# A decode block's down projection in row form over four column groups, with its residual kept as four rows

## The chip, the cores and the metric

One core of one Trainium2 chip. The metric is the device time of one execution in microseconds (us), lowest is best. The program is one launch. Inside an execution, the profile gives times from the start of the span. All runs quoted here are in the fast state unless said otherwise; executions of the kernel before lie between 412.1 and 412.9 us, apart from occasional ones at 413.1 to 413.8 us (see the last experiments), so differences of 0.1 to 0.3 us between times say little by themselves.

Some words used below: a *packet* is one record of a DMA engine (for a large load, one partition's row); a load is *usable* at the last increment of its semaphore; *PE* is TensorE, *DVE* VectorE, *ACT* ScalarE, *SPq* the queue of SyncE; the *granted clock* is the share of TensorE's full clock that the profile shows.

## The reference

One token goes through a pre-layernorm attention block with a cached KV of 65,536 positions and then a gated feed-forward block:

```python
h  = x + attention(layernorm(x), k_cache, v_cache, wq, wo)   # 32 query heads, 4 KV heads, Dh = 128
h2 = h + (gelu(layernorm(h) @ w_gate) * (layernorm(h) @ w_up)) @ w_down   # D = 1024, F = 3584
```

Everything is bfloat16 in memory. 173 MB are read once, of which 134 MB are the two caches and 22 MB the three feed-forward matrices. The output is one row of 1024 values.

## The kernel before

All large tensors pass through five rotating load buffers of 32 KB a partition, filled by one queue (SyncE's). The tail of the kernel, which the change rewrites:

```python
def load(src, name):                       # every large load: one DMA into a rotating buffer
    t = chpool.tile([P, CW], BF16, name=name, tag="ch")      # 5 buffers of 32768 bytes a partition
    ...
x_row = const.tile([DC, P], BF16, name="x_row")              # x as 8 rows, transposed to x_cp at the start
...
def pair_mm(bank, stat, w2, c, first, last):                 # two 512-column matmuls of a row block
    for s in range(DS):
        g = 2 * s + c % 2
        nc.tensor.matmul(bank[32 * g:32 * g + 32, :], lhsT=stat, rhs=w2[:, s * 512:(s + 1) * 512],
                         start=first, stop=last, tile_position=(0, 32 * g))
...
h_cp = cp_sum(at_r, x_cp, "h_cp")          # residual in column form: h[j*128+p] in partition p, column j
...
for sz in [14, 7, 4, 2, 1]:                # down weights: 28 row blocks in 5 loads
    wv = load(wd_v[:, c0:c0 + sz, :], "wd_sb")
    for cc in range(sz):
        c = c0 + cc
        if c < 14:
            pair_mm(d_ps, actz[:, c, :], wv[:, cc, :], c, c < 2, c + 2 >= 14)
            continue
        for j in range(8):                 # weights stationary, one column moving
            nc.tensor.matmul(dl_ps[:, j:j + 1], lhsT=wv[:, cc, j * P:(j + 1) * P], rhs=act_bf[:, c:c + 1], ...)
    if c0 == 14:                           # after the first load: rows to columns, plus the residual
        nc.vector.tensor_copy(out=d_r[:], in_=d_ps[:])
        hd_cp = cp_sum(d_r, h_cp, "hd_cp")
h2_cp = dl_ps + hd_cp                      # then transpose to 8 rows, cast, one store of 8 rows
nc.sync.dma_start(out=out[0, 0].rearrange("(c p) -> c p", p=P), in_=o_row[:])
```

Of the kernel before, what the change touches and what calls it, by code (L numbers as in the profile page):

```python
# [9 lines left out]
ALU = mybir.AluOpType  # L10
AX = mybir.AxisListType
BF16 = mybir.dt.bfloat16
F32 = mybir.dt.float32
# [4 lines left out]
def kernel(  # L18
# [13 lines left out]
    nc = tc.nc  # L32
    P = 128
    D = A_x.shape[-1]
# [5 lines left out]
    DC = D // P  # L40
    FC = F // P
# [18 lines left out]
    const = ctx.enter_context(tc.tile_pool(name="const", bufs=1))  # L60
    small = ctx.enter_context(tc.tile_pool(name="small", bufs=2))
    chpool = ctx.enter_context(tc.tile_pool(name="chpool", bufs=NBUF))
    ps_m = ctx.enter_context(tc.tile_pool(name="ps_m", bufs=1, space=PSUM))
# [10 lines left out]
    def load(src, name):  # L74
        t = chpool.tile([P, CW], BF16, name=name, tag="ch")
        n, w = src.shape[1], src.shape[2]
        tv = t[:, 0:n * w].rearrange("p (n w) -> p n w", w=w)
        nc.sync.dma_start(out=tv, in_=src)
        return tv
# [3 lines left out]
    assert HD <= CW and DC % WB == 0  # L83
    x_pc_bf = const.tile([P, DC], BF16, name="x_pc_bf")
    nc.scalar.dma_start(out=x_pc_bf[:], in_=A_x[0, 0].rearrange("(p c) -> p c", c=DC))
    x_row = const.tile([DC, P], BF16, name="x_row")
    nc.scalar.dma_start(out=x_row[:], in_=A_x[0, 0].rearrange("(c p) -> c p", p=P))
    wq_tiles = []
    for c0 in range(0, DC, WB):
        wv = load(wq_v[:, c0:c0 + WB, :], "wq_sb")  # L90
        wq_tiles.extend(wv[:, i, :] for i in range(WB))

    ident_bf = const.tile([P, P], BF16, name="ident_bf")
    make_identity(nc, ident_bf[:])
    ident_f = const.tile([P, P], F32, name="ident_f")
# [3 lines left out]
    hsel = const.tile([P, 2], F32, name="hsel")  # L99
# [43 lines left out]
    nc.vector.tensor_copy(out=x_pc[:], in_=x_pc_bf[:])  # L143
    xn_bf = const.tile([P, DC], BF16, name="xn_bf")
    layernorm_cols(x_pc[:], xn_bf[:], "ln1")
    xT_ps = ps_m.tile([P, DC], BF16, name="xT_ps", tag="misc")
    nc.tensor.transpose(out=xT_ps[:], in_=x_row[:], identity=ident_bf[0:DC, 0:DC])
    x_cp = const.tile([P, DC], F32, name="x_cp")
    nc.vector.tensor_copy(out=x_cp[:], in_=xT_ps[:])

    def padded(pool, vec, ncols, name):
        t = pool.tile([P, ncols, 32], BF16, name=name)
        nc.gpsimd.memset(t[:], 0.0)
        nc.vector.tensor_copy(out=t[:, :, 0], in_=vec)
        return t

    def wide_mm(banks, stat, mov, ns, first, last):
        for s in range(ns):
            g = s % 4
            nc.tensor.matmul(banks[s // 4][32 * g:32 * g + 32, :], lhsT=stat, rhs=mov(s),  # L160
                             start=first, stop=last, tile_position=(0, 32 * g))

    def evac(dst, src, k):
        if k % 2 == 0:
            nc.vector.tensor_copy(out=dst, in_=src)  # L165
        else:
            nc.scalar.copy(out=dst, in_=src)  # L167
# [20 lines left out]
    for hf in range(2):  # L188
        for t in range(2):
            o = W2 * hf + rep * t  # L190
            nc.vector.tensor_copy(out=qsel[64 * t:64 * t + 64, :, :, hf, o:o + rep],
                                  in_=qsel_ps[64 * t:64 * t + 64, :, :].rearrange("p a (g h) -> p g a h", h=rep))
# [149 lines left out]
    for dq in range(OQ):  # L342
        nc.tensor.matmul(o2_ps[:], lhsT=osel[:, dq, :], rhs=o_sb[:, dq * Hq:(dq + 1) * Hq],
                         start=(dq == 0), stop=(dq == OQ - 1))

    actx.close()
    rows = ctx.enter_context(tc.tile_pool(name="rows", bufs=1))
    ps_w = ctx.enter_context(tc.tile_pool(name="ps_w", bufs=4, space=PSUM))
    ps_t = ctx.enter_context(tc.tile_pool(name="ps_t", bufs=3, space=PSUM))
    DS = D // 512  # L350

    def row_bank(name):
        return ps_w.tile([P, 512], F32, name=name, tag="w")

    def pair_mm(bank, stat, w2, c, first, last):
# [4 lines that stand above are left out]
# [6 lines left out]
    for wc in range(Hq // WN):  # L366
        wv = load(wo_v[:, wc * WN:(wc + 1) * WN, :], "wo_sb")
        for cc in range(WN):
            c = wc * WN + cc
            pair_mm(at_ps, o2z[:, c, :], wv[:, cc, :], c, c < 2, c + 2 >= Hq)  # L370
    at_r = rows.tile([P, 512], F32, name="at_r")
    nc.vector.tensor_copy(out=at_r[:], in_=at_ps[:])
    hc_ps = ps_t.tile([P, DC], F32, name="hc_ps", tag="T")
    for s in range(DS):
        for c in range(DC):
            nc.tensor.matmul(hc_ps[64 * s:64 * s + 64, c:c + 1], lhsT=at_r[:, c::DC], rhs=hsel[:, s:s + 1],
                             start=True, stop=True, tile_position=(0, 64 * s))
# [3 lines left out]
    layernorm_cols(h_pc[:], hn_bf[:], "ln2")  # L381
    hnz = padded(rows, hn_bf[:], DC, "hnz")

    def cp_sum(row, add, name):
        ps = ps_t.tile([P, 4, DS], F32, name=name + "_ps", tag="T")
        for b in range(4):
            nc.tensor.matmul(ps[:, b, :], lhsT=row[:, b * P:(b + 1) * P], rhs=hsel[:], start=True, stop=True)
        t = rows.tile([P, DC], F32, name=name)
        nc.vector.tensor_tensor(out=t[:].rearrange("p (s b) -> p b s", b=4), in0=ps[:],
                                in1=add[:].rearrange("p (s b) -> p b s", b=4), op=ALU.add)  # L390
        return t

    h_cp = cp_sum(at_r, x_cp, "h_cp")

    assert F <= CW and FC == 28
    GB = CW // F
    NF = FC // 4

    def up_proj(wmat, name, sizes):
        banks = [row_bank(name + "_ps") for _ in range(2)]  # L400
        wv_all = wmat.rearrange("(p c) n -> p c n", c=DC)
        c0 = 0
        for sz in sizes:
            wv = load(wv_all[:, c0:c0 + sz, :], name + "_sb")
            for cc in range(sz):
                c = c0 + cc
                wide_mm(banks, hnz[:, c, :],
                        lambda s, w=wv[:, cc, :]: w.rearrange("p (m j) -> p m j", j=FC)[:, :, 4 * s:4 * s + 4],
                        NF, c == 0, c == DC - 1)
            c0 += sz  # L410
        assert c0 == DC
        outs = []
        for k in range(2):
            ng = min(4, NF - 4 * k)
            ev = rows.tile([P, 512], F32, name=name + "_ev", tag=f"ev{k}")
            evac(ev[0:32 * ng, :], banks[k][0:32 * ng, :], k)
            t_ps = ps_t.tile([P, 4, P], F32, name=name + "_t", tag="T")
            for b in range(4):
                nc.tensor.transpose(out=t_ps[:, b, 0:32 * ng], in_=ev[0:32 * ng, b::4],
                                    identity=ident_f[0:32 * ng, 0:32 * ng])  # L420
            outs.append((16 * k, 4 * ng, t_ps[:, :, 0:32 * ng:32]))
        return outs

    def by_j(t, j0, nj):
        return t[:, j0:j0 + nj].rearrange("p (g b) -> p b g", b=4)
# [11 lines left out]
    gl = rows.tile([P, FC], F32, name="gl")  # L437
    nc.vector.tensor_tensor(out=gl[:], in0=th[:], in1=g_ap[:], op=ALU.mult)
    act_bf = rows.tile([P, FC], BF16, name="act_bf")
    for j0, nj, src in up_proj(B_w_up, "wu", [GB] * (DC // GB - 1) + [GB - 1, 1]):  # L440
        nc.vector.tensor_tensor(out=by_j(act_bf, j0, nj), in0=src, in1=by_j(gl, j0, nj), op=ALU.mult)

    wd_v = B_w_down.rearrange("(p c) n -> p c n", p=P)
    sizes = [14, 7, 4, 2, 1]
    assert sum(sizes) == FC
    NW = sizes[0]
    actz = padded(rows, act_bf[:, 0:NW], NW, "actz")
    d_ps = row_bank("d_ps")
    dl_ps = ps_w.tile([P, DC], F32, name="dl_ps", tag="w")
    nc.vector.memset(dl_ps[:], 0.0)  # L450
    c0 = 0
    for sz in sizes:
        wv = load(wd_v[:, c0:c0 + sz, :], "wd_sb")
        for cc in range(sz):
            c = c0 + cc
            if c < NW:
                pair_mm(d_ps, actz[:, c, :], wv[:, cc, :], c, c < 2, c + 2 >= NW)
                continue
            for j in range(DC):
                nc.tensor.matmul(dl_ps[:, j:j + 1], lhsT=wv[:, cc, j * P:(j + 1) * P], rhs=act_bf[:, c:c + 1],  # L460
                                 start=False, stop=False, skip_group_check=True)
        c0 += sz
        if c0 == NW:
            d_r = rows.tile([P, 512], F32, name="d_r")
            nc.vector.tensor_copy(out=d_r[:], in_=d_ps[:])
            hd_cp = cp_sum(d_r, h_cp, "hd_cp")
    h2_cp = rows.tile([P, DC], F32, name="h2_cp")
    nc.vector.tensor_tensor(out=h2_cp[:], in0=dl_ps[:], in1=hd_cp[:], op=ALU.add)
    h2T_ps = ps_t.tile([DC, P], F32, name="h2T_ps", tag="T")
    nc.tensor.transpose(out=h2T_ps[:], in_=h2_cp[:], identity=ident_f[:])  # L470
    o_row = rows.tile([DC, P], BF16, name="o_row")
    nc.vector.tensor_copy(out=o_row[:], in_=h2T_ps[:])
    nc.sync.dma_start(out=out[0, 0].rearrange("(c p) -> c p", p=P), in_=o_row[:])


# [28 lines left out]
```

## Time and profile before

412.35 us (three runs, 412.24 to 412.71); the profiled execution took 412.36 us, its span is 410.5 us.

| what | reading | where |
|---|---|---|
| load queue busy | 98.1% of 16 DMA engines' span, 422 GB/s | queue table of the page |
| last down weights usable | 406.89 us | last semaphore increment of that load |
| last down matmul ends | 407.33 us | chain |
| store issued, duration of the issue | 408.34 us, 0.348 us | timeline |
| result landed | 409.55 us | last semaphore increment of the store |

The page of the kernel before: the DMA rows of its 40 slices (tenths of busy time, then GB/s), the packet counts and the load queue (packets, MB, share of 16 engines).

```profile
DMA  8999999999999999999999999999999999999994
GB/s 358 409 460 407 460 408 457 407 454 414 439 428 429 434 417 449 416 449 410 449 420 441 423 441 426 431 433 426 437 426 437 422 445 422 434 430 433 429 418 174
DMA packets 6828, 173.43 MB, mean 422 GB/s; under 512 B 912, under 2 KB 912, under 8 KB 1296
q1 hardware_dynamic: 6640, 173.02, 98.1%
```

DMA is at 8 or 9 tenths from the first slice to the last but one: the kernel is as long as its load stream, plus what follows the last bytes. What follows them is in the timeline of the kernel before, without its weight-load lines and one small add (start us, duration us, engine, line, operation, output from inputs, count, and in brackets the idle time before it and what ended it):

```profile
398.43 3.18 PE L358 MATMUL d_ps<-wd_sb,actz 128*32 128x512 bf16 x28 [5.03 <-DMA wd_sb<-in_B_w_down_dram]
401.66 0.69 DVE L465 COPY d_r<-d_ps 128x512 f32<-128x512 f32 x1 [8.02 <-PE d_ps L358]
402.40 1.86 PE L387 MATMUL hd_cp_ps<-hsel,d_r 128*128 128x2 f32 x8 [0.79 <-DVE d_r L465]
404.13 3.19 PE L460 MATMUL dl_ps<-act_bf,wd_sb 128*128 128x1 bf16 x112
407.35 0.17 DVE L468 TENSOR_TENSOR h_cp<-dl_ps,hd_cp 128x8 f32<-128x8 f32 x1 [2.87 <-PE dl_ps L460]
407.57 0.38 PE L470 MATMUL h2T_ps<-ident_f,h_cp 128*8 128x128 f32 x1 [0.26 <-DVE h_cp L468]
407.99 0.28 DVE L472 CAST o_row<-h2T_ps 8x128 bf16<-8x128 f32 x1 [0.47 <-PE h2T_ps L470]
408.34 0.35 SPq L473 DMA_DIRECT2D out_dram<-o_row  x1
```

Four hand-overs, add, TensorE transpose, cast, store issue, lie between the last down matmul and the store.

### The profile page before, as it was taken

How to read it: one execution, taken by the hardware profiler on the slowest of the kernel's cores; microseconds unless marked ns; L12 is line 12 of the kernel's file. 1: busy time of each engine (PE TensorE's matmuls, PEld its weight loads, DVE VectorE, ACT ScalarE, POOL GpSimd, SP SyncE). 2: the span in 40 equal slices, each digit the busy share in tenths (PEclk: the TensorE clock that was granted, in tenths of full speed). 3: DMA queues.
4: the chain of work that ended last, by engine and by line, in shares of the span. 5: the costliest groups of instructions: out<-in, count | busy, mean ns of one | idle time of the engine just before them, and what ended most of it. 6: DMA issues, size and time to landing. Idle time of an engine off the chain costs nothing.

```text
span 410.5 us, 6349 instructions
## 1 busy us (share of the span) xinstructions
PE 297.7 (73%) x2705; PEld 195.3 (48%) x2705; DVE 167.6 (41%) x292; ACT 168.0 (41%) x281; POOL 5.1 (1%) x16
## 2 busy tenths in 40 slices
PE   0438989889688987496988929888987466466546
PEld 0216656655365654464565617465654223163225
DVE  0213565557256545265556535456545101021011
ACT  0013766653855654733655634455754700000000
POOL 1100000000000000000000000000000001000000
PEclk9986999999999999599999966999999585568565
DMA  8999999999999999999999999999999999999994
GB/s 358 409 460 407 460 408 457 407 454 414 439 428 429 434 417 449 416 449 410 449 420 441 423 441 426 431 433 426 437 426 437 422 445 422 434 430 433 429 418 174
DMA packets 6828, 173.43 MB, mean 422 GB/s; under 512 B 912, under 2 KB 912, under 8 KB 1296
## 3 DMA queue, kind: packets, MB, share of 16 engines
q1 hardware_dynamic: 6640, 173.02, 98.1%
q8 instruction: 21, 0.34, 0.3%
q14 instruction: 7, 0.06, 0.0%
q10 hardware_dynamic: 160, 0.00, 0.0%
HBM read 173.02 MB, written 0.00 MB: 422 GB/s over the span
## 4 chain that ended last, share of the span: by engine, by line
PE 51%; DMA 20%; DVE 14%; issue 8%; ACT 6%; POOL 0%; SPq 0%; POOLq 0%; ACTq 0%; DVEq 0%
PE kt_ps L220 26%; PE qk_ps L245 11%; DMA k_sb<-in_A_k_cache_dram 7%; DMA wd_sb<-in_B_w_down_dram 6%; DMA v_sb<-in_A_v_cache_dram 6%; DVE sc_sb L256 5%; PE acc_ps L300 5%; ACT pT L283 4%; PE sct_ps L253 4%; DVE mx L257 4%; DVE kt_sb L227 3%; ACT qk_sb L250 2%; PE o_ps L316 1%; PE wg_ps L160 1%; PE d_ps L358 1%
## 5 line engine op out<-in xcount | busy, mean ns | idle before, releaser
L220 PE MATMUL kt_ps<-ident_f,k_sb 128*128 128x128 f32 x1024 | 148.1, 288 | 17.4 <-DVE kt_sb L227 13.0
L225 ACT COPY kt_sb<-kt_ps 128x1024 bf16<-128x1024 bf16 x116 | 116.4, 1013 | 91.7 <-PE kt_ps L220 63.0
L220 PEld LDWEIGHTS kt_ps<-ident_f,k_sb 128*128 128x128 f32 x1024 | 117.5, 147 | 55.5 <-issue 21.3
L227 DVE COPY kt_sb<-kt_ps 128x1024 bf16<-128x1024 bf16 x140 | 94.6, 687 | 76.1 <-PE qk_ps L245 42.6
L245 PE MATMUL qk_ps<-kt_sb,qsel 128*32 128x512 bf16 x512 | 65.1, 395 | 7.7 <-DVE kt_sb L227 7.7
L256 DVE COPY sc_sb<-sct_ps 128x512 f32<-128x512 f32 x32 | 34.2, 1068 | 46.1 <-PE sct_ps L253 43.7
L283 ACT ACTIVATE pT<-sc_sb,nbias 128x256 bf16<-128x256 f32 x64 | 31.5, 493 | 20.6 <-DVE nbias L275 20.6
L300 PE MATMUL acc_ps<-v_sb,pT 128*32 128x512 bf16 x512 | 33.7, 407 | 3.7 <-DMA v_sb<-in_A_v_cache_dram 3.7
L250 ACT COPY qk_sb<-qk_ps 128x512 f32<-128x512 f32 x32 | 18.8, 589 | 24.9 <-PE qk_ps L245 16.5
L245 PEld LDWEIGHTS <-qsel 128*32 128x32 bf16 x512 | 15.1, 94 | 26.2 <-issue 23.8
L253 PE MATMUL sct_ps<-ident_f,qk_sb 128*128 128x128 f32 x128 | 19.9, 278 | 8.6 <-ACT qk_sb L250 8.6
L300 PEld LDWEIGHTS <-pT 128*32 128x32 bf16 x512 | 14.7, 102 | 18.5 <-issue 7.1
L257 DVE TENSOR_REDUCE mx<-sc_sb 128x8 f32<-128x512 f32 x32 | 22.0, 686 | 1.0
L253 PEld LDWEIGHTS sct_ps<-ident_f,qk_sb 128*128 128x128 f32 x128 | 14.3, 140 | 13.6 <-ACT qk_sb L250 13.6
L167 ACT COPY wg_ev<-wg_ps 96x512 f32<-96x512 f32 x1 | 0.6, 581 | 45.9 <-PE wg_ps L160 45.9
L309 PE MATMUL l_ps<-lpart,ones_f 128*128 128x8 f32 x16 | 3.7, 306 | 15.8 <-ACT pT L283 15.8
L358 PE MATMUL at_ps<-wo_sb,o2z 128*32 128x512 bf16 x64 | 7.1, 619 | 8.1 <-DMA wo_sb<-in_A_wo_dram 8.1
L160 PE MATMUL wu_ps<-wu_sb,hnz 128*32 128x512 bf16 x56 | 7.2, 625 | 7.8 <-DMA wu_sb<-in_B_w_up_dram 7.8
L160 PEld LDWEIGHTS <-hnz 128*32 128x32 bf16 x112 | 4.8, 123 | 16.0 <-issue 13.7
L283 ACT ACTIVATION_READ_ACCUMULATOR pT<-sc_sb,nbias 128x1 f32 x64 | 11.9, 187 | 0.0
L167 ACT ACT_TABLE_LOAD x1 | 1.3, 1283 | 25.0 <-DVE q_ev L165 25.0
L309 PEld LDWEIGHTS l_ps<-lpart,ones_f 128*128 128x128 f32 x16 | 3.0, 234 | 17.8 <-ACT pT L283 17.4
(126 smaller groups left out, 98.4 us busy)
## 6 DMA issues: line engine op xcount, KB each, us to landing
k_sb<-in_A_k_cache_dram SPq DMA_DIRECT2D x16, 4096.0 KB, 30.4
v_sb<-in_A_v_cache_dram SPq DMA_DIRECT2D x16, 4096.0 KB, 19.3
wq_sb<-in_A_wq_dram SPq DMA_DIRECT2D x2, 4096.0 KB, 16.7
wo_sb<-in_A_wo_dram SPq DMA_DIRECT2D x2, 4096.0 KB, 29.6
wg_sb<-in_B_w_gate_dram SPq DMA_DIRECT2D x2, 3584.0 KB, 36.4
wu_sb<-in_B_w_up_dram SPq DMA_DIRECT2D x1, 3584.0 KB
wd_sb<-in_B_w_down_dram SPq DMA_DIRECT2D x1, 3584.0 KB, 25.6
wu_sb<-in_B_w_up_dram SPq DMA_DIRECT2D x1, 2688.0 KB, 38.1
```

Source lines behind the costliest of these rows:

```text
L160: nc.tensor.matmul(banks[s // 4][32 * g:32 * g + 32, :], lhsT=stat, rhs=mov(s), start=first, stop=last, tile_position=(0, 32 * g))
L220: nc.tensor.transpose(out=kt_ps[:, b, :], in_=k32s[m0 // 16][:, m0 % 16, :], identity=ident_f[:])
L225: nc.scalar.copy(out=dst_bf, in_=src_bf)
L227: nc.vector.tensor_copy(out=dst_bf, in_=src_bf)
L245: nc.tensor.matmul(qk_ps[32 * c:32 * c + 32, :], lhsT=qsel[:, g, par, hf, :], rhs=mv[:, :, :, par], start=(hf == 0 and par == 0), stop=(hf ...
L250: nc.scalar.copy(out=qk_sb[:], in_=qk_ps[:])
L253: nc.tensor.transpose(out=sct_ps[:, b, :], in_=qk_sb[:, b * P:(b + 1) * P], identity=ident_f[:])
L256: nc.vector.tensor_copy(out=sl.rearrange("p h (m t) -> p m t h", t=2), in_=src_v)
L257: nc.vector.tensor_reduce(out=st["mx"][:, :, pi], in_=sl, axis=AX.X, op=ALU.max)
L283: nc.scalar.activation(out=pT[:, :, r, :], in_=sc_sb[:, r, hf * HG * TG:(hf + 1) * HG * TG].rearrange("p (a t) -> p a t", t=TG), func=ACT. ...
L300: nc.tensor.matmul(acc[32 * c:32 * c + rep * TG, :], lhsT=pTs[a // HG][:, a % HG, :, :].rearrange("p r t -> p (r t)"), rhs=v_sb[:, i * TG: ...
L358: nc.tensor.matmul(bank[32 * g:32 * g + 32, :], lhsT=stat, rhs=w2[:, s * 512:(s + 1) * 512], start=first, stop=last, tile_position=(0, 32 ...
```

## The change

Its intent: drop the mixed form. All 28 row blocks of the down projection become four matmuls of 256 outputs each, one in each of the four 32-column groups of the array, which run side by side. The result then lies as four rows of 256 in partitions 0, 32, 64 and 96; the residual is kept in the same layout, so one add of 97x256 and one store of four rows end the kernel. The up weights come in two loads and not three.

```diff
-    x_row = const.tile([DC, P], BF16, name="x_row")
-    nc.scalar.dma_start(out=x_row[:], in_=A_x[0, 0].rearrange("(c p) -> c p", p=P))
+    NQD = D // 4
+    x4 = const.tile([P, NQD], BF16, name="x4")
+    nc.gpsimd.memset(x4[:], 0.0)
+    nc.scalar.dma_start(out=x4[0:P:32, :], in_=A_x[0, 0].rearrange("(q n) -> q n", q=4))
...
-    xT_ps = ...; x_cp = const.tile([P, DC], F32, name="x_cp")      (transpose of x_row)
...
-    h_cp = cp_sum(at_r, x_cp, "h_cp")
+    (h4_ps and h4 are allocated, h4_ps is cleared)
+    for q in range(4):
+        nc.tensor.matmul(h4_ps[32 * q:32 * q + 1, :], lhsT=hsel[:, q // 2:q // 2 + 1],
+                         rhs=at_r[:, (q % 2) * NQD:(q % 2 + 1) * NQD], start=True, stop=True, tile_position=(0, 32 * q))
+    nc.vector.tensor_tensor(out=h4[:], in0=h4_ps[:], in1=x4[:], op=ALU.add)
...
-    for j0, nj, src in up_proj(B_w_up, "wu", [GB] * (DC // GB - 1) + [GB - 1, 1]):
+    for j0, nj, src in up_proj(B_w_up, "wu", [GB] * (DC // GB)):
...
-            (pair_mm for the first 14 blocks, 8 one-column matmuls for the others, cp_sum between)
+    (d_ps is now 128x256 and is cleared)
+            for q in range(4):
+                nc.tensor.matmul(d_ps[32 * q:32 * q + 1, :], lhsT=act_bf[:, c:c + 1],
+                                 rhs=wv[:, cc, q * NQD:(q + 1) * NQD], start=(c == 0), stop=(c == FC - 1),
+                                 tile_position=(0, 32 * q))
...
-    (add, transpose, cast, store of 8 rows)
+    nc.vector.tensor_tensor(out=o4[0:97, :], in0=d_ps[0:97, :], in1=h4[0:97, :], op=ALU.add)
+    nc.sync.dma_start(out=out[0, 0].rearrange("(q n) -> q n", q=4), in_=o4[0:P:32, :])
```

More of the change, by code (lines that the diff above doesn't have):

```diff
@@ L145 @@
     layernorm_cols(x_pc[:], xn_bf[:], "ln1")
-    xT_ps = ps_m.tile([P, DC], BF16, name="xT_ps", tag="misc")
-    nc.tensor.transpose(out=xT_ps[:], in_=x_row[:], identity=ident_bf[0:DC, 0:DC])
-    x_cp = const.tile([P, DC], F32, name="x_cp")
-    nc.vector.tensor_copy(out=x_cp[:], in_=xT_ps[:])
     def padded(pool, vec, ncols, name):
@@ L382 @@
     hnz = padded(rows, hn_bf[:], DC, "hnz")
-    def cp_sum(row, add, name):
-        ps = ps_t.tile([P, 4, DS], F32, name=name + "_ps", tag="T")
-        for b in range(4):
-            nc.tensor.matmul(ps[:, b, :], lhsT=row[:, b * P:(b + 1) * P], rhs=hsel[:], start=True, stop=True)
-        t = rows.tile([P, DC], F32, name=name)
-        nc.vector.tensor_tensor(out=t[:].rearrange("p (s b) -> p b s", b=4), in0=ps[:],
-                                in1=add[:].rearrange("p (s b) -> p b s", b=4), op=ALU.add)
-        return t
-    h_cp = cp_sum(at_r, x_cp, "h_cp")
+    h4_ps = ps_t.tile([P, NQD], F32, name="h4_ps", tag="T")
+    nc.vector.memset(h4_ps[:], 0.0)
+    for q in range(4):
+        nc.tensor.matmul(h4_ps[32 * q:32 * q + 1, :], lhsT=hsel[:, q // 2:q // 2 + 1],
+                         rhs=at_r[:, (q % 2) * NQD:(q % 2 + 1) * NQD], start=True, stop=True, tile_position=(0, 32 * q))
+    h4 = rows.tile([P, NQD], F32, name="h4")
+    nc.vector.tensor_tensor(out=h4[:], in0=h4_ps[:], in1=x4[:], op=ALU.add)
     assert F <= CW and FC == 28
@@ L445 @@
     assert sum(sizes) == FC
-    NW = sizes[0]
-    actz = padded(rows, act_bf[:, 0:NW], NW, "actz")
-    d_ps = row_bank("d_ps")
-    dl_ps = ps_w.tile([P, DC], F32, name="dl_ps", tag="w")
-    nc.vector.memset(dl_ps[:], 0.0)
+    d_ps = ps_w.tile([P, NQD], F32, name="d_ps", tag="w")
+    nc.vector.memset(d_ps[:], 0.0)
     c0 = 0
@@ L455 @@
             c = c0 + cc
-            if c < NW:
-                pair_mm(d_ps, actz[:, c, :], wv[:, cc, :], c, c < 2, c + 2 >= NW)
-                continue
-            for j in range(DC):
-                nc.tensor.matmul(dl_ps[:, j:j + 1], lhsT=wv[:, cc, j * P:(j + 1) * P], rhs=act_bf[:, c:c + 1],
-                                 start=False, stop=False, skip_group_check=True)
-        c0 += sz
-        if c0 == NW:
-            d_r = rows.tile([P, 512], F32, name="d_r")
-            nc.vector.tensor_copy(out=d_r[:], in_=d_ps[:])
-            hd_cp = cp_sum(d_r, h_cp, "hd_cp")
-    h2_cp = rows.tile([P, DC], F32, name="h2_cp")
-    nc.vector.tensor_tensor(out=h2_cp[:], in0=dl_ps[:], in1=hd_cp[:], op=ALU.add)
-    h2T_ps = ps_t.tile([DC, P], F32, name="h2T_ps", tag="T")
-    nc.tensor.transpose(out=h2T_ps[:], in_=h2_cp[:], identity=ident_f[:])
-    o_row = rows.tile([DC, P], BF16, name="o_row")
-    nc.vector.tensor_copy(out=o_row[:], in_=h2T_ps[:])
-    nc.sync.dma_start(out=out[0, 0].rearrange("(c p) -> c p", p=P), in_=o_row[:])
+            for q in range(4):
+                nc.tensor.matmul(d_ps[32 * q:32 * q + 1, :], lhsT=act_bf[:, c:c + 1],
+                                 rhs=wv[:, cc, q * NQD:(q + 1) * NQD], start=(c == 0), stop=(c == FC - 1),
+                                 tile_position=(0, 32 * q))
+        c0 += sz
+    o4 = rows.tile([P, NQD], BF16, name="o4")
+    nc.vector.tensor_tensor(out=o4[0:97, :], in0=d_ps[0:97, :], in1=h4[0:97, :], op=ALU.add)
+    nc.sync.dma_start(out=out[0, 0].rearrange("(q n) -> q n", q=4), in_=o4[0:P:32, :])
 _INS = ['A_x', 'A_k_cache', 'A_v_cache', 'A_wq', 'A_wo', 'B_x', 'B_w_gate', 'B_w_up', 'B_w_down']
```

## The prediction

> **What bounds the kernel now.** The load stream: the slices of the span show DMA at 8 or 9 tenths throughout, the queue table has the load queue at 98.1% of 16 engines' span (173.02 MB, 422 GB/s). Only what follows the last weight bytes is left to gain. In one-microsecond windows the DMA share falls from 0.97 (402 to 403 us) to 0.15 (406 to 407); the last completion packet is at 406.58, so the data are usable at about 406.7 (first down load: 398.30, matmul at 398.43).
>
> The chain of waits at the end: d_ps matmuls at 398.43 for 3.20, eviction of 128x512 0.69, row-to-column matmuls 1.86 (at 402.40), 112 one-column matmuls 404.13 to 407.33, 26.7 ns apart without a pause, add 0.17, transpose 0.38, cast 0.28, store issued at 408.34, span end 410.5.
>
> **What the change does, costed.**
>
> 1. The last 14 row blocks: 8 matmuls a block (0.21 us) become 4 of 256 columns in four column groups. In the trace four 512-column ones start together, the next four 0.427 us later (granted clock 0.50), so about 0.213 us a block: no throughput gained. The Trainium skill (TensorE: Matmul & The Clock Gate, Back-to-back issue gap) says N/1.2 ns cold, which agrees at 512.
> 2. The mid-tail detour (eviction 0.69, row-to-column 1.86) goes. Today TensorE is late for the last block and ends 0.6 us after its landing; after, it should wait for each load and start the last block at about 406.7. An isolated 256-column matmul costs (219+N)/1.2 = 0.40 us by the same page (Single matmul latency); the trace has 0.585 to 0.607 at 512, where that gives 0.609. End about 407.1 instead of 407.33: 0.2 us.
> 3. Add, transpose, cast and hand-overs (407.35 to 408.34) become one add of 97x256 from PSUM. From 128x512 in 0.69 and 128x8 in 0.17 us I estimate 1.03 ns a column, 0.43 us, store about 0.06 later: 0.5 us less. A 4-row store instead of 8: landing unchanged.
> 4. Up weights in two loads: the second chunk's 28 matmuls begin when all 3584 KB are in (about 390 instead of 387.8); act_bf is ready at 395.5 to 396 instead of 393.6. The first down load lands at 398.4: hidden. The queue stays fed (down loads are issued 15 to 28 us before landing).
> 5. h_cp (8 matmul records, 1.87 us) becomes 4 float32 matmuls of 256 columns and an add of 128x256, perhaps 2 us, beside the second layernorm; TensorE has 4.7 us idle before the up weights at 381.2: hidden, like the x transpose in the head.
>
> So of some 6 us of removed work, about 0.7 us lies on the critical path.
>
> **Prediction.** 411.65 us, 8 in 10 between 411.0 and 412.3. Faster by over 2%: 0.01; within 2%: 0.98; slower by over 2%: 0.01.
>
> **What would show it.** Right: DMA share and GB/s as before; TensorE waits at each down load; the last matmul ends within 0.45 us of the last completion packet; last add 0.4 to 0.5 us; act_bf about 2 us later yet before the first down load lands. Wrong: no wait at the last down loads (the four-group form slower than 0.213 us a block), or a wait for act_bf at the first down matmul.
>
> **What would make it wrong.** One-column weight loads serialising the four groups; the 16 DMA engines ending the stream more or less evenly (now between 405.1 and 406.6), which can shift the end by half a microsecond; another granted clock in the tail.

## The result

414.28 us (median of four runs, 414.24 to 414.45), against 412.39 us for the kernel before in the same rounds (412.24 to 412.71): ratio 1.0046, 95% interval 1.0028 to 1.0063. Here and below a ratio is the mean time of one kernel's fast runs over that of the other's of the same rounds, so it is not quite the ratio of the medians. The change is slower by 1.9 us, clear of noise, where a gain of 0.7 us was forecast, and the time lies outside the stated range.

The page of the changed kernel, the lines that answer to those of before:

```profile
DMA  8999999999999999999999999999999999999993
GB/s 356 410 454 412 451 408 452 405 455 408 443 419 440 421 432 428 429 434 427 434 427 435 427 429 434 424 436 418 442 415 444 413 450 413 427 436 434 419 420 154
DMA packets 6668, 173.43 MB, mean 420 GB/s; under 512 B 872, under 2 KB 880, under 8 KB 1136
q1 hardware_dynamic: 6488, 173.02, 98.0%
```

The same bytes, the queue as busy as before, fewer packets, and yet 420 GB/s instead of 422. Half a per cent of 410 us is 2 us. The timeline of its tail, without the weight-load lines:

```profile
400.31 3.15 PE L448 MATMUL d_ps<-wd_sb,act_bf 128*1 128x256 bf16 x56 [3.35 <-DMA wd_sb<-in_B_w_down_dram]
404.63 1.66 PE L448 MATMUL d_ps<-wd_sb,act_bf 128*1 128x256 bf16 x28 [1.17 <-DMA wd_sb<-in_B_w_down_dram]
407.10 1.02 PE L448 MATMUL d_ps<-wd_sb,act_bf 128*1 128x256 bf16 x16 [0.80 <-DMA wd_sb<-in_B_w_down_dram]
408.37 1.04 PE L448 MATMUL d_ps<-wd_sb,act_bf 128*1 128x256 bf16 x12 [0.25 <-DMA wd_sb<-in_B_w_down_dram]
409.46 0.42 DVE L453 TENSOR_TENSOR o_4079<-d_ps,h_3786 97x256 bf16<-97x256 f32 x1 [12.27 <-PE d_ps L448]
409.95 0.66 SPq L454 DMA_DIRECT2D out_dram<-o_4079  x1
```

TensorE does what was predicted: it waits for the loads (the last four matmuls, merged into the line of 408.37, start at 409.02), takes 3.15 us for 14 blocks, and one add of 0.42 us follows. But the first down load is usable at 400.26 us instead of 398.39, so the loss is made before this tail begins. Two things are new: the whole stream is late, and the issue of the store takes 0.66 us where it took 0.35.

Where does the stream fall behind? The DMA records of the two traces give the time at which so many megabytes had arrived:

```
MB arrived      20      62      104     146     170     173.3
before, us     49.67  146.70  244.01  341.61  396.71  405.13
after, us      49.73  147.21  244.94  342.58  398.35  407.07
difference     +0.06   +0.51   +0.93   +0.97   +1.64   +1.93
```

It falls behind a little at a time, from early on, through stages whose instructions the change does not touch. The durations of single packets say how. The first three rows are of packets of 32,768 bytes that start after 45 us (one partition's row of a load):

```
                                      before    after
median, ns                             1213      1216
share that took over 1213 ns           1.3%     99.8%
mean without those over 1290 ns, ns   1213.0    1217.8
packets of 28,672 bytes, median, ns    1062      1066
all packets, summed, over 16, us      404.26    405.85
```

Nearly every one of these packets takes longer, 84% of them by 3 to 11 ns. The sum of all packet times, divided by the 16 DMA engines, grows by 1.59 us, most of the 1.93 us by which the last bytes are late. The changed kernel's packets are at 1213 ns too until about 32 us of the span; from 36 us on more than half are slower, from 50 us on nearly all, to the end.

### The profile page after: what moved, and what is told of

Same layout as the page of the kernel before. It is cut to its first block, busy times and chain, and to the rows that moved or that the text cites. A ratio compares the mean times of both kernels' runs of the same rounds, so it can differ in the third digit from the quotient of the medians.

```text
span 412.5 us, 6266 instructions
## 1 busy us (share of the span) xinstructions
PE 296.2 (72%) x2667; PEld 190.3 (46%) x2667; DVE 167.2 (41%) x288; ACT 168.1 (41%) x281; POOL 5.0 (1%) x16
## 4 chain that ended last, share of the span: by engine, by line
PE 49%; DMA 29%; DVE 13%; ACT 6%; issue 2%; SPq 0%; ACTq 0%; DVEq 0%
PE kt_ps L217 27%; PE qk_ps L242 11%; DMA wu_sb<-in_B_w_up_dram 10%; DMA wo_sb<-in_A_wo_dram 8%; DMA k_sb<-in_A_k_cache_dram 7%; DVE sc_sb L253 5%; PE acc_ps L297 5%; PE sct_ps L250 4%; ACT pT L280 4%; DVE mx L254 4%; DMA wd_sb<-in_B_w_down_dram 3%; DVE kt_sb L224 3%; ACT qk_sb L247 2%; PE wu_ps L157 1%; PE at_ps L355 1%
```

## The experiments

What in the change can make every packet slower, through stages that it does not touch? The load buffers are allocated behind the constants and the small tiles. The change takes out `x_row` (256 bytes a partition) and `x_cp` (32 bytes) and puts in `x4` (512 bytes), so everything behind moves by 512 - 256 - 32 = 224 bytes. In the built programs the first load buffer begins at byte 23552 of each partition before (a multiple of 512) and at 23776 after (a multiple of 32, not of 64).

**Theory A**: the address at which a load writes is what costs. **Rival B**: one of the new instructions does, for instance the load of x into partitions 0, 32, 64 and 96, which leaves the queues in some slower state. Two runs tell them apart: the changed kernel with its buffers moved back, and the kernel before with its buffers moved.

### e1: the changed kernel, buffers back on a multiple of 512

```diff
+    pad_t = padpool.tile([P, 144], BF16, name="pad_t")     # 288 bytes, ahead of the load buffers
+    nc.gpsimd.memset(pad_t[:, 0:1], 0.0)
```

> The changed kernel with one unused tile of 288 bytes a partition ahead of the load buffers, so that these begin at a multiple of 512 bytes again (24064) instead of 224 past one (23776), and everything behind them with them. Theory A (the shifted SBUF addresses cost the load stream 3 to 5 ns in every 32 KB packet, and so 1.6 to 1.9 us over the run): median 32 KB packet back from 1216 to 1213 ns, the last completion packet near 406.6 us of the span instead of 408.5, time 412.2 to 412.7. Rival B (the strided 4-row load of x, or another new instruction, leaves the DMA queues in a slower state): packets stay at 1216 ns and the time at 414.2 to 414.5.

Measured: 412.18 us (four runs, 412.0 to 412.82), ratio to before 0.9992 (0.9978 to 1.0007). Median packet 1213 ns. The last completion packet in its profile (407.23, the load usable at 407.56) is later than the 406.6 expected, for that execution was the long one of the four (412.82); e13 below repeats the kernel, with 406.59 and 406.90.

### e2: the kernel before, buffers moved by 224 bytes

```diff
+    pad_t = padpool.tile([P, 112], BF16, name="pad_t")     # 224 bytes
```

> The kernel before with one unused tile of 224 bytes a partition ahead of the load buffers, so that these and everything behind them lie 224 bytes past a multiple of 512, as in the changed kernel. Theory A: packets of 32 KB at 1216 ns from about 35 us on, time 413.9 to 414.4, about 1.8 us slower than before. Rival B: 1213 ns and 412.4.

Measured: 414.47 us (414.45 to 414.5), ratio 1.0045 (1.003 to 1.006). Median packet 1216 ns, 100.0% of those after 45 us over 1213. An unused tile of 224 bytes costs the kernel before as much as the whole change does. Rival B falls.

The stretch from 45 to 250 us, where the attention runs, in the kernel before, in e2, in the changed kernel and in e13 (e1 again): from:to, length, busy time and instructions of PE, PEld, DVE, ACT and POOL, granted clock, DMA share, GB/s.

```profile
45.00:250.00 205.00, 165.82 (x1469) 112.06 (x1468) 110.27 (x165) 116.14 (x197) 0.00 (x0) 0.95 1.01 432
```

```profile
45.00:250.00 205.00, 165.86 (x1468) 112.05 (x1467) 110.30 (x165) 116.26 (x198) 0.00 (x0) 0.95 1.00 430
```

```profile
45.00:250.00 205.00, 165.49 (x1466) 111.50 (x1465) 109.83 (x165) 115.75 (x196) 0.00 (x0) 0.95 1.00 430
```

```profile
45.00:250.00 205.00, 165.46 (x1467) 111.41 (x1466) 110.10 (x164) 115.67 (x195) 0.00 (x0) 0.95 1.00 431
```

The engines do the same work, within 0.6 per cent, at the same clock. The GB/s go down with the shift, but a step of 1 in this view is coarse; the packets' durations are the finer measure.

### e3 and e4: which of the moved tiles

In the changed kernel and in e2 the slow packets begin at about 32 us, close to the first key transposes (32.5 us). So the tiles behind the load buffers, which VectorE and ScalarE write then, could be the ones that matter. Two runs with a second pad behind the load buffers move one group and not the other.

```diff
# e3: changed kernel       load buffers on a multiple of 512, the tiles behind 224 past one
+    pad_t  288 bytes ahead of the load buffers;  pad_t2  224 bytes behind them
# e4: kernel before        load buffers 224 past a multiple of 512, the tiles behind on one
+    pad_t  224 bytes ahead of the load buffers;  pad_t2  288 bytes behind them
```

> The changed kernel with the load buffers on a multiple of 512 bytes, but the tiles behind them (transposed keys, scores, probabilities) still 224 past one. The slow packets begin at about 33 us, when the first key transposes and copies start, so the tiles that the engines write could be what matters. Theory A1 (the address at which a load writes matters): 1213 ns, 412.2 to 412.7. Theory A2 (the addresses of the tiles behind matter): 1216 ns, 414.0 to 414.5.

Measured: 412.33 us (412.1 to 413.46), 1213 ns.

> The kernel before with the load buffers 224 bytes past a multiple of 512 and the tiles behind them on one. A1: 1216 ns, 413.9 to 414.4. A2: 1213 ns, 412.4. Rival B (neither address matters): 412.4 here and in the other run of the kernel before.

Measured: 414.64 us (414.54 to 414.74), 1216 ns. It is the address of the load buffers (A1), not that of the tiles that the engines write. (In both runs the tiles of the stages after the attention follow the load buffers; but those are used 300 us after the packets have become slow.)

### e5, e6, e9, e10: how much alignment

The Trainium skill has a candidate for the size: "DMA: Bandwidth & Descriptors", section "How a descriptor splits into AXI transactions", says that a descriptor is cut into transactions of 256 bytes that start at 256-byte boundaries, and that the first transaction of one which starts off a boundary begins at the boundary below, with unused bytes. The page tells it of reads; here it is the written side that moved. Four runs of the kernel before with a pad of 32, 64, 128 and 256 bytes:

```diff
+    pad_t = padpool.tile([P, 16 | 32 | 64 | 128], BF16, name="pad_t")
```

> The kernel before with 32 unused bytes a partition ahead of the load buffers: they lie 32 bytes past a multiple of 512 (and so of 64). If what costs is a write address that is no multiple of 64 bytes: 1216 ns a 32 KB packet and 414.2 to 414.7, as with 224. If the loss grows with the distance from a 512-byte line: clearly less than with 224.

> The kernel before with 64 unused bytes ahead of the load buffers: 64 past a multiple of 512. If a multiple of 64 bytes is enough: 1213 ns and 412.2 to 412.7. If a multiple of 128, 256 or 512 bytes is needed: 1216 ns and 414.2 to 414.7.

> The kernel before with the load buffers 128 bytes past a multiple of 512 (32, 64 and 224 past it gave medians of 1216, 1215 and 1216 ns a 32 KB packet and 414.4 to 414.7 us). If a multiple of 128 bytes is enough: 1213 ns and 412.2 to 412.7. If 256 or 512 is needed: 1214 to 1216 ns and 414.0 to 414.7.

> The same with 256 bytes past a multiple of 512. If 128 or 256 is enough: 1213 ns and 412.2 to 412.7. If the load buffers have to begin on a multiple of 512: 1214 to 1216 ns and 414.0 to 414.7.

```
bytes past a multiple of 512     0      32      64      128     224     256
time, us (median)             412.35  414.66  414.36  414.01  414.47  412.60
32 KB packet, median ns         1213    1216    1215    1216    1216    1213
share of these over 1213 ns     1.3%   97.6%   92.3%   76.6%  100.0%    1.4%
sum of packets over 16, us    404.26  406.04  405.60  405.60  405.93  403.98
last down load usable, us     406.89  409.19  408.76  408.70  409.13  407.07
```

The packets are those that start after 45 us. A multiple of 256 bytes is enough and 128 is not: 412.6 against 414.0. Off it, the loss depends little on the distance: 1.7 to 2.2 us against the kernel before of the same rounds, least at 128, where a quarter of the packets stay at 1213 ns. The boundary agrees with the page's 256 bytes. Its mechanism is not shown: by the page's two unaligned examples a read costs one beat (32 bytes) more at 32 bytes past the boundary and seven more at 224, while here both lose 3 ns in the median.

### e7, e8, e12: the store of four rows

With aligned buffers the changed kernel is level with the one before, and the 0.7 us of gain is still missing. The issue of its store stands out, so three runs cut it up.

```diff
# e7: aligned changed kernel, four one-row stores, two on each queue
-    nc.sync.dma_start(out=..., in_=o4[0:P:32, :])
+    for q in range(4):
+        eng = nc.sync if q % 2 == 0 else nc.scalar
+        eng.dma_start(out=out_q[q:q + 1, :], in_=o4[32 * q:32 * q + 1, :])
# e8: kernel before, its 8 adjacent rows as 4 on SyncE's queue and 4 on ScalarE's
# e12: aligned changed kernel, two stores of two rows 32 partitions apart, one on each queue
+    nc.sync.dma_start(out=out_q[0:2, :], in_=o4[0:64:32, :])
+    nc.scalar.dma_start(out=out_q[2:4, :], in_=o4[64:P:32, :])
```

> The changed kernel with aligned load buffers, the result stored as four one-row stores, two on SyncE's queue and two on ScalarE's, in place of one store of four rows that lie 32 partitions apart. That one takes 0.657 us to issue and lands 1.67 us after its issue began; the 8 adjacent rows of the kernel before take 0.348 and land 1.21 after. If the stride is what makes the issue slow, each one-row store issues in about 0.35 us, the second of a queue lands about 1.55 to 1.6 us after the first began, and the time is about 0.1 us under the aligned kernel's 412.18: 412.0 to 412.15. If the small number of rows makes it slow, each takes 0.6 us or more and the time is 412.5 or longer.

Measured: 412.52 us (412.36 to 413.57). The one-row stores issue in 0.25 to 0.32 us each, so the rows are not too few; but the last of the four lands 1.65 us after the first issue began, as the single store's 1.67. So there is no gain at the landing; the expected 0.1 us is too small to be read from the times.

> The kernel before, its 8 adjacent result rows stored as 4 on SyncE's queue and 4 on ScalarE's. If the stride of 32 partitions makes the changed kernel's store slow to issue: each issues in about 0.35 us, landing 1.2 us after, time 412.3 to 412.6 as before. If it is that a store has only 4 rows: 0.65 us, and the time 412.7 to 413.0.

Measured: 412.73 us (412.25 to 412.9), ratio 1.0002 (0.9987 to 1.0017). Four adjacent rows issue in 0.28 and 0.35 us; the last lands 1.36 us after the first issue began, where 1.2 was expected. So it is the stride of 32 partitions, not the four rows, that makes an issue slow.

> The aligned changed kernel with the store cut into two of two rows each, 32 partitions apart, one on SyncE's queue and one on ScalarE's. If the slow issue of a strided store (0.657 us for 4 rows) grows with the rows, each takes about 0.4 us, the last lands 1.35 to 1.45 us after the first issue began instead of 1.67, and the time falls by about 0.2 us, to 411.9 to 412.3. If it is a fixed price of a strided store: 0.65 us each, landing at 1.67, no gain.

Measured: 412.47 us (412.33 to 412.51). The issues take 0.57 and 0.63 us with half the rows each: nearly a fixed price of a strided store. The last lands 1.94 us after the first issue began, later than the single store.

### e11, e13, e14, e15: are the two up loads hidden?

```diff
# e11 and e14: aligned changed kernel     up_proj(B_w_up, "wu", [GB] * (DC // GB - 1) + [GB - 1, 1])
# e13: e1 again, as their partner
# e15: kernel before                      up_proj(B_w_up, "wu", [GB] * (DC // GB))
```

> The aligned changed kernel with the up weights in three loads again. The prediction called the two-load part hidden. If it is: act_bf about 2 us earlier, the first down matmul still waiting for its load, and the time equal to the aligned kernel's 412.18 within the 0.3 us by which runs differ. If the two loads cost or gain something in the load stream: a difference of 0.5 us or more, with a matching shift of the last load's landing.

Measured: 413.56 us (executions 413.58, 414.02, 412.72, 413.54). This looked like a cost of 1.4 us, and it is not readable: in the profiled execution six 32 KB packets that start between 264.8 and 265.4 us of the span take 1.9 to 2.2 us and several after them 1.3 to 1.7, 75 us before any up load is issued. The long execution of e1 (412.82) shows the same stretch, those of the kernel before (412.36) and of e7 do not. In the traces of e1, e3, e11, e16 and e17 the arrived bytes fall about 1 us further behind those of the kernel before between 112 and 116 MB (263 to 272 us), so the stretch is most of what makes these executions long. So e11 was run again beside its partner.

> The aligned changed kernel once more, with 5 rounds, as the partner of the next runs. 412.0 to 412.3 in the executions without a stretch of long packets, 0.8 us more in those with one.

Measured: 412.44 us (executions 412.25, 412.5, 412.44, 412.19, 413.23), two of the lower four 0.14 to 0.2 us above the range expected.

> The aligned changed kernel with the up weights in three loads. If that part is hidden, as predicted: the lower executions within 0.2 us of the partner's lower ones. If three loads cost something here: 412.6 to 412.8 at the lowest, as the one low execution of the first try (412.72) suggests, and the last down load lands later by as much.

Measured: 412.52 us (412.52, 412.3, 413.66, 412.4, 413.4). The ratio to the kernel before is 1.0014 (1.0001 to 1.0027) with the two long executions in it, the partner's 1.0004 (0.9992 to 1.0016). Its lower executions, 412.3 to 412.5, are those of its partner, although the profiled one (412.52) has a weaker stretch of long packets at 264.5 us.

> The kernel before with nothing changed but the up weights in two loads. Hidden: 412.2 to 412.6, as before, act_bf about 2 us later and still ahead of the first down load. If two loads gain: 0.3 us or more under the kernel before of the same rounds.

Measured: 412.28 us (412.25 to 412.38), ratio 0.9998 (0.9986 to 1.001); the activations (act_bf) are ready at 395.33 us instead of 393.64, and the last down load is usable at 406.89 us, to the hundredth as before. The two-load part is hidden, as predicted.

### e16: the store without its stride, with a wrong result

```diff
-    nc.sync.dma_start(out=out[0, 0].rearrange("(q n) -> q n", q=4), in_=o4[0:P:32, :])
+    nc.sync.dma_start(out=out[0, 0].rearrange("(q n) -> q n", q=4), in_=o4[0:4, :])      # wrong rows
```

> A wrong result on purpose: the aligned changed kernel stores the adjacent partitions 0 to 3 in place of 0, 32, 64 and 96, so only the first quarter of the output is right. It takes the stride of the store away and nothing else. If the stride costs what the trace shows: issue 0.33 to 0.35 us, landing 1.2 us after the issue began instead of 1.67, and 0.4 to 0.5 us under the partner: 411.6 to 411.8. If the stride is not the cause: within 0.15 us of the partner.

Measured: wrong; 412.28 us median, but of six executions between 411.64 and 413.73 (413.39, 411.64, 411.65, 412.01, 412.55, 413.73). The median can't be read; the two lowest, 411.64 and 411.65, are 0.55 us below the lowest of the partner (412.19). Their traces were not taken; the profiled execution shows the issue and the landing. The timelines, first of e13, then of e16 (whose profiled execution is a long one, so its loads landed 1.6 us later):

```profile
407.38 0.43 DVE L456 TENSOR_TENSOR o<-d_ps,h 97x256 bf16<-97x256 f32 x1 [12.06 <-PE d_ps L451]
407.88 0.66 SPq L457 DMA_DIRECT2D out_dram<-o  x1
```

```profile
408.98 0.42 DVE L456 TENSOR_TENSOR o<-d_ps,h 97x256 bf16<-97x256 f32 x1 [12.10 <-PE d_ps L451]
409.48 0.34 SPq L457 DMA_DIRECT2D out_dram<-o  x1
```

The tail of each, counted from the last increment of the last down load's semaphore, all in us:

```
                               before    after    e13     e16
last down load usable          406.89   408.98   406.90  408.51
store issued after that          1.45     0.97     0.98    0.97
store landed after its issue     1.21     1.67     1.67    1.20
span ends after that             0.93     0.83     0.83    0.83
```

The new tail gains 0.47 us up to the store's issue and gives 0.46 us back between issue and landing. Without the stride it would keep it. (The last row is no effect of the change: other runs of the aligned kernel, e11 and e14, have 0.93 there too, and e15, a run of the kernel before, has 0.83.)

### e17: a right result without the stride

A last try to keep the gain: the weights stationary for all 28 blocks, but with output 8p+j in partition p and column j, by taking every eighth weight column. The residual in that layout exists already (h_pc), one add of 128x8 follows, and the store has 128 adjacent partitions. Buffers are on a multiple of 256.

```diff
+            for j in range(DC):
+                nc.tensor.matmul(dl_ps[:, j:j + 1], lhsT=wv[:, cc, j::DC], rhs=act_bf[:, c:c + 1], ...)
+    nc.vector.tensor_tensor(out=o_pc[:], in0=dl_ps[:], in1=h_pc[:], op=ALU.add)
+    nc.sync.dma_start(out=out[0, 0].rearrange("(p c) -> p c", c=DC), in_=o_pc[:])
```

> A version made from the kernel before: the whole down projection in the form of its last 14 blocks (weights stationary, one-column matmuls), but with output 8p+j in partition p and column j, by taking every eighth weight column. The residual is then h_pc, which the second layernorm needs anyway; one add of 128x8 (0.17 us) ends the computation and the store has 128 adjacent partitions. Load buffers on a multiple of 256 bytes. If weight columns 16 bytes apart load as fast as adjacent ones (26.7 ns each, 0.21 us a block): store issued 0.44 + 0.17 + 0.1 = 0.7 us after the last landing (1.45 before, 0.98 changed), landed 1.2 to 1.3 later, time 411.5 to 411.8. If they load slower (say 100 ns each, 0.85 us a block): the last block costs 0.65 us more and the time is 412.2 to 412.6.

Measured: right, 416.76 us (416.32 to 417.21), slower by 4.3 us. Its timeline:

```profile
399.28 13.62 PE L439 MATMUL dl_ps<-act_bf,wd_sb 128*128 128x1 bf16 x224 [6.22 <-DMA wd_sb<-in_B_w_down_dram]
412.94 0.17 DVE L443 TENSOR_TENSOR o_pc<-dl_ps,h_pc 128x8 bf16<-128x8 f32 x1 [19.64 <-PE dl_ps L439]
413.18 0.35 SPq L444 DMA_DIRECT2D out_dram<-o_pc  x1
```

The 224 matmuls, whose weights lie in columns 16 bytes apart, take 13.62 us, 60 ns from one start to the next, where adjacent columns took 26.7. That is the expectation's slower case; its 100 ns was too high, but all 28 blocks pay and not only the last, so that the time is 4 us over the range given. The loads had landed by 407.73, so TensorE is 5 us late. The end itself is as short as hoped: the store is issued 0.28 us after the last matmul ends. No version that was run beats both kernels: the aligned changed kernel is level with the kernel before (ratios 0.9992 and 1.0004).

## Why the prediction was wrong

- **"DMA share and GB/s as before"**: this is the step that failed. The prediction costed instructions and took the load stream for a constant. The stream went from 422 to 420 GB/s, its 32 KB packets from 1213 to 1216 ns in the median, and its last load was usable at 408.98 instead of 406.89 us, because a constant tile grew and pushed the load buffers off a multiple of 256 bytes. Shown by e1 to e4 (moving the buffers alone takes the loss away or makes it, about 2 us either way) and sized by e5, e6, e9 and e10. None of the stated ways to be wrong named it; "the 16 DMA engines ending the stream more or less evenly" was nearest.
- **Point 1, 0.213 us a block, no throughput gained**: right. From the second block on, the groups of four start 0.213 us apart (granted clock 0.50). The Trainium skill's N/1.2 ns ("TensorE: Matmul & The Clock Gate", "Back-to-back issue gap") agrees. The isolated matmul of 256 columns was put at 0.40, an estimate from that page's formula, which is for a full array of 128 weight columns and was used here for one: the records of the first four after a wait have 0.37 us, those within a stream 0.42.
- **Point 2, 0.2 us because "TensorE is late for the last block"**: wrong in size, it is nothing. The last down load was usable at 406.89, not at 406.7: the prediction took the last completion packet plus the 0.13 us of another load, where the semaphore's own increments give the time. The kernel before wasn't late either: its last eight matmuls have a pause of 65 ns ahead of them, which the prediction read as none, and begin 0.05 us after the landing. TensorE ended 0.44 us after that landing before, and 0.45 in e13. The detour of 2.6 us was wholly hidden.
- **Point 3, one add of 0.43 us, 0.5 us less up to the store**: right, 0.42 us and 0.47 (e13, 0.98 against 1.45 us from the last landing). **"Landing unchanged"**: wrong, 1.67 against 1.21 us. The prediction looked at rows and bytes of the store and not at its stride. This mis-sized term alone takes the rest of the gain (e16).
- **Point 4 and point 5, hidden**: right for the up loads (e15). The residual's matmuls and add (8 matmul records and 0.42 us of VectorE) lie in a stage where the up weights are still to come; from the start of the eviction of at_r to the start of the copy that makes hnz, the input of the gate matmuls, there are 9.64 us before (359.22 to 368.86) and 9.51 after (361.25 to 370.76), so it is hidden there; no run measured it alone.

So of the forecast 0.7 us, 0.2 did not exist, 0.47 came and 0.46 was lost in the store, and 1.9 us were lost in the stream. What stays open: why the packets of the moved buffers are at 1213 ns for the first 32 us and longer. The point from which more than half are slow isn't fixed to the first key transposes: it lies at 35 us in the changed kernel, e2 and e5, at 39 in e4, 44 in e6 and 47 in e9. Nor does an engine have to be at work at that moment, for late in the changed kernel, while TensorE, VectorE and ScalarE are idle from 386.9 to 391.7 us, packets of 28,672 bytes stay at 1066 ns; more than that no run tells.

## What to carry to other kernels

When a kernel is bound by its loads, look up where its load buffers lie after any change to the tiles ahead of them, and keep them on a multiple of 256 bytes, the smallest step that was enough here; a difference of a fraction of a per cent in GB/s with unchanged bytes is the sign, and the durations of packets of one size are the evidence. A pad of a few bytes ahead of the buffers is the test, on both kernels. Count the end of a kernel to the landing of its result, not to the issue of its store: here rows that lie 32 partitions apart cost between issue and landing what their layout had saved before it.

## What the Trainium skill lacked or had wrong

- "DMA: Bandwidth & Descriptors", "How a descriptor splits into AXI transactions", tells the 256-byte boundary of what a descriptor reads. The runs show a 256-byte boundary for the address in SBUF that a load writes, too (1213 ns a 32 KB packet on a multiple of 256, 1215 to 1216 off it), and what it costs: 1.7 to 2.2 us of 412. Its rules for kernel authors do not have it.
- "SBUF — State Buffer", "Operand start alignment", gives element size as the rule for where a tile may start and says "This is about legality, not speed". The runs time it for loads: starts that are a multiple of 32, 64 or 128 bytes only lose 1.7 to 2.2 us of 412.
- No page gives the price of a store from partitions that are not adjacent: 0.65 to 0.66 us of issue for four rows and 0.57 to 0.63 for two, against 0.28 to 0.37 for four or eight adjacent rows.
- "SBUF — State Buffer" has lines of 16 bytes and says that each access which crosses to a new line pays a penalty; it gives no figure, and no page times it for weight loads. Weights from columns 16 bytes apart took 60 ns a matmul against 26.7 ns (e17); that the lines are the reason is not shown.
- No page has the stretch of long packets near 265 us (32 KB packets of up to 3.3 us, several at once) that makes some executions about 1 us longer. The kernel before has long executions too (5 of 11 beside e17 were at 413.1 to 413.8 us), but their traces were not taken. Its cause is open.
